# Attention and MLP of one gated block: one hand-ordered stream of work in place of three stages

## The chip, the cores and the metric

One core of one Trainium2 chip runs the kernel. The metric is the device time of one execution in microseconds. Engines are named as the profile names them: PE (matrix products), DVE (vector), ACT (activation functions), POOL and SP (here they mostly issue DMAs). PSUM is the memory that PE writes its products to; SBUF is the working memory.

## What is computed

The input x has 2048 tokens of 512 values, all tensors are bf16. Its LayerNorm goes into two branches, and the product of both is added to x:

```python
x = A_x
xn = _layernorm(x, axis=-1)
s = _A_ref(xn, A_k_cache, A_v_cache, A_wq, A_wo)
g = _silu(_B_ref(xn, B_w1, B_w2))
return x + s * g
```

Branch A is attention: q = xn @ wq gives 32 heads of 128; every 4 heads share one of 8 heads of the K and V caches, of which the last W = 512 positions are used, without a mask; scores are scaled by 128 ** -0.5, a softmax follows, p @ v, and the joined heads (4096 values) go through wo to 512 values. Branch B is an MLP: silu(xn @ w1) with 1792 inner values, then @ w2, and silu once more on the result.

## The kernel before

The 2048 tokens are four blocks of 512 (`NBLK`), each of four tiles of 128 (`BLKT`). The kernel has three stages, each with its own tile pools, and a scheduler orders the instructions of each engine.

- Start (lines 81 to 131): 16 tiles of x, K, V, w1, w2, wq and wo are loaded on SP's and POOL's queues. K is turned by PE transposes into `kT` (line 103), copied out of PSUM by DVE (104). Each tile of x gets its LayerNorm (113 to 120: statistics, a square root on ACT, reciprocal, centre and scale), four PE transposes (130) and a DVE copy (131) into `xnT`.
- MLP (133 to 166): for each block 14 products `h_ps` of four matmuls (143), a sigmoid on ACT (151) and a multiply on DVE (152) into `hT`; then for each of four tiles 14 matmuls `oB_ps` (157), sigmoid (165) and multiply (166) into `g_sb`. Both PSUM tiles have two buffers.
- Attention (168 to 240): for each block and each of 32 heads four matmuls give `qT_ps` (180), DVE casts it to `qT_s` (188); for each of four tiles one matmul gives the scores `sc_ps` of 128 by 512 (192), ACT takes exp into `e_t` and sums the row into `den` (197), DVE takes the reciprocal (199) and writes the scaled row into `p_all` (200), a view in pieces of 128. One transposing DMA on SP's queue turns `p_all` into `pT_sb` (206), four matmuls with V give `oT_ps` (212), DVE casts it into `oT_store` (219). `p_all` and `pT_sb` have two buffers, `qT_ps` and `oT_ps` one each, `sc_ps` three. After the heads of a block come four sums of 32 matmuls each, `s_ps` (224), two buffers; the scheduler lets two of them begin beside the block's heads. Their results are multiplied by `g_sb` (235), added to x (239) and stored (240).

In every matmul of the MLP, the attention and the output, 512 columns are streamed against a weight of 128 by 128.

## Time and profile before

| | us |
|---|---|
| median of 6 runs (757.45 to 763.96) | 759.74 |
| the profiled execution | 759.4 |
| its span, first to last instruction | 757.6 |
| PE busy, 2592 matmuls | 605.5 |
| DVE busy | 480.5 |
| ACT busy | 371.4 |

The span is what the trace covers; the profiled execution's own time is 1.8 us longer. Engines run beside one another, so their busy times don't add up to the span. Matmuls overlap, so their pitch, start to start, tells more than the duration of one (about 380 ns). A line such as L212 is line 212 of the kernel before. In the views of the trace "x4" is a count, "idle before" is time in which the engine stood still ahead of the instruction, and the name behind "<-" is what ended that wait. The chain of waits goes back from the last instruction to what released it, step by step; "issue" is time in which it found nothing to wait for. For DMAs, "to landing" runs from the issue to the arrival of all bytes.

### The profile page before, as it was taken

Reading aid. Unit: us, or ns where it says so; the run is one execution under the profiler, and the core shown is the slowest. Engines: PE = TensorE matmul, PEld = TensorE weight load, DVE = VectorE, ACT = ScalarE, POOL = GpSimd, SP = SyncE. Lnnn points to the kernel's source line nnn. Section 1 sums busy time; section 2 is a strip of 40 time slices with the busy share of each in tenths; the row PEclk is TensorE's granted clock in tenths of the full one; section 3 lists DMA queues with packets and bytes.
Section 4 is the critical chain, followed back from the end, with each engine's and each line's share of the span. In section 5 each row is a group of like instructions: output and inputs, shape, how many; then the busy total and the mean of one; then the engine's idle time right before and its main releaser. Section 6 shows DMA issues by size and latency. Waiting matters only on the chain.

```text
span 757.6 us, 8922 instructions
## 1 busy us (share of the span) xinstructions
PE 605.5 (80%) x2592; PEld 244.2 (32%) x2592; DVE 480.5 (63%) x1473; ACT 371.4 (49%) x1115; POOL 22.6 (3%) x40
## 2 busy tenths in 40 slices
PE   1049999988989889787777898887887978877866
PEld 1033444433333334233232343333232422323322
DVE  3274445547868763676767747767676477777741
ACT  1015344447767650565656525666565256656520
POOL 7000000000000000000000000000000100000000
PEclk9999999999999999999999999999999999999979
DMA  9960000008787883676777665667767367667740
GB/s 278 349 232 0 1 0 1 1 24 157 148 137 148 152 142 73 104 133 125 126 122 129 114 122 108 129 118 133 123 123 135 92 114 136 127 127 125 132 81 27
DMA packets 278064, 88.13 MB, mean 116 GB/s; under 512 B 271424, under 2 KB 274496, under 8 KB 277504
## 3 DMA queue, kind: packets, MB, share of 16 engines
q1 hardware_dynamic: 274976, 77.35, 54.2%
q0 software_dynamic: 3040, 10.23, 4.0%
q8 instruction: 20, 0.33, 0.2%
q14 instruction: 28, 0.23, 0.1%
HBM read 18.35 MB, written 2.10 MB: 27 GB/s over the span
## 4 chain that ended last, share of the span: by engine, by line
issue 40%; PE 25%; DMA 25%; DVE 7%; ACT 2%; POOL 1%; SPq 0%; POOLq 0%; DVEq 0%; ACTq 0%
DMA pT_sb<-p_all 20%; PE oB_ps L157 6%; PE h_ps L143 6%; PE oT_ps L212 4%; PE s_ps L224 3%; DMA k_nat<-in_A_k_cache_dram 3%; PE sc_ps L192 3%; PE qT_ps L180 2%; DMA w_sb<-in_B_w_dram 2%; DVE p_all L200 1%; DVE oT_store L219 1%; DVE qT_s L188 1%; ACT e_t L197 1%; PE xnT_ps L130 1%; DVE xnT L131 1%
## 5 line engine op out<-in xcount | busy, mean ns | idle before, releaser
L197 ACT ACTIVATE e_t<-sc_ps 128x512 bf16<-128x512 f32 x512 | 300.7, 596 | 241.7 <-PE sc_ps L192 207.1
L192 PE MATMUL sc_ps<-kT,qT_s 128*128 128x512 bf16 x512 | 160.5, 383 | 34.5 <-DVE qT_s L188 32.5
L200 DVE TENSOR_SCALAR p_all<-e_t,rden 128x512 bf16<-128x512 bf16 x512 | 172.5, 350 | 23.9 <-DMA pT_sb<-p_all 14.7
L212 PE MATMUL oT_ps<-pT_sb,v_sb 128*128 128x512 bf16 x512 | 133.9, 384 | 51.3 <-DMA pT_sb<-p_all 49.8
L180 PE MATMUL qT_ps<-xnT,wq_sb 128*128 128x512 bf16 x512 | 146.8, 382 | 2.0 <-DVE g_sb L166 1.4
L224 PE MATMUL s_ps<-wo_sb,oT_store 128*128 128x512 bf16 x512 | 136.0, 385 | 11.6 <-DVE oT_store L219 10.7
L199 DVE RECIPROCAL rden<-den 128x1 f32<-128x1 f32 x512 | 77.2, 160 | 74.1 <-ACT e_t L197 70.5
L219 DVE CAST oT_store<-oT_ps 128x512 bf16<-128x512 f32 x128 | 88.1, 688 | 36.0 <-PE oT_ps L212 35.5
L197 ACT ACTIVATION_READ_ACCUMULATOR e_t<-sc_ps 128x1 f32 x512 | 103.5, 202 | 0.0
L188 DVE CAST qT_s<-qT_ps 128x512 bf16<-128x512 f32 x128 | 87.1, 681 | 11.3 <-PE qT_ps L180 9.7
L212 PEld LDWEIGHTS <-v_sb 128*128 128x128 bf16 x512 | 49.7, 97 | 125.3 <-issue 83.8
L192 PEld LDWEIGHTS <-qT_s 128*128 128x128 bf16 x512 | 47.2, 98 | 120.5 <-DVE qT_s L188 72.4
L224 PEld LDWEIGHTS <-oT_store 128*128 128x128 bf16 x512 | 48.4, 99 | 81.9 <-DVE oT_store L219 27.9
L180 PEld LDWEIGHTS <-wq_sb 128*128 128x128 bf16 x512 | 50.3, 98 | 70.8 <-issue 17.9
L143 PE MATMUL h_ps<-xnT,w_sb 128*128 128x512 bf16 x224 | 55.0, 386 | 3.7 <-DVE hT L152 3.2
L152 DVE TENSOR_TENSOR hT<-h_ps,sig 128x512 bf16<-128x512 f32 x56 | 38.6, 691 | 29.9 <-ACT sig L151 29.9
L157 PE MATMUL oB_ps<-w_sb,hT 128*128 128x512 bf16 x224 | 53.2, 379 | 0.3 <-DVE g_sb L166 0.3
L151 ACT ACTIVATE sig<-h_ps 128x512 bf16<-128x512 f32 x56 | 33.4, 597 | 31.3 <-PE h_ps L143 31.3
L235 DVE TENSOR_TENSOR sg<-s_ps,g_sb 128x512 f32<-128x512 f32 x16 | 10.7, 688 | 41.5 <-PE s_ps L224 41.5
L143 PEld LDWEIGHTS <-w_sb 128*128 128x128 bf16 x224 | 22.0, 98 | 33.5 <-issue 10.7
L157 PEld LDWEIGHTS <-hT 128*128 128x128 bf16 x224 | 21.2, 98 | 28.1 <-DVE hT L152 2.9
L166 DVE TENSOR_TENSOR g_sb<-oB_ps,sig 128x512 bf16<-128x512 f32 x16 | 11.1, 692 | 26.6 <-ACT sig L165 26.6
(30 smaller groups left out, 106.5 us busy)
## 6 DMA issues: line engine op xcount, KB each, us to landing
wo_sb<-in_A_wo_dram POOLq DMA_DIRECT2D x1, 4096.0 KB, 34.5
wq_sb<-in_A_wq_dram SPq DMA_DIRECT2D x1, 4096.0 KB, 31.6
pT_sb<-p_all SPq DMA_TRANSPOSE x128, 4.3
w_sb<-in_B_w_dram SPq DMA_DIRECT2D x1, 1792.0 KB, 13.8
w_sb<-in_B_w_dram POOLq DMA_DIRECT2D x1, 1792.0 KB, 12.7
x_t<-in_A_x_dram SPq DMA_DIRECT2D x8, 128.0 KB, 14.1
x_t<-in_A_x_dram POOLq DMA_DIRECT2D x8, 128.0 KB, 7.7
x_e<-in_A_x_dram SPq DMA_DIRECT2D x8, 128.0 KB, 2.2
```

The source lines that it names most:

```text
L143: nc.tensor.matmul(h_ps, w1_sb[:, c, f * P : (f + 1) * P], xnT[:, c, tok0 : tok0 + BLK], start=(c == 0), stop=(c == ND - 1),)
L152: nc.vector.tensor_tensor(out=hT[:, f, :], in0=h_ps, in1=sig, op=ALU.mult)
L157: nc.tensor.matmul(oB_ps, hT[:, f, j * P : (j + 1) * P], w2_sb[:, f, :], start=(f == 0), stop=(f == NFC - 1),)
L180: nc.tensor.matmul(qT_ps, wq_sb[:, c, h * DH : (h + 1) * DH], xnT[:, c, tok0 : tok0 + BLK], start=(c == 0), stop=(c == ND - 1),)
L188: nc.vector.tensor_copy(qT_s, qT_ps)
L192: nc.tensor.matmul(sc_ps, qT_s[:, j * P : (j + 1) * P], kT[:, g_kv, :], start=True, stop=True)
L197: nc.scalar.activation(e_t, sc_ps, ACT.Exp, scale=INV_SQRT_DH, accum_out=den)
L199: nc.vector.reciprocal(rden, den)
L200: nc.vector.tensor_scalar_mul(p_all[:, :, j, :], e_t.rearrange("p (kc q) -> p kc q", q=P), rden,)
L212: nc.tensor.matmul(oT_ps, v_sb[:, g_kv, kc, :], pT_sb[:, kc, :], start=(kc == 0), stop=(kc == NKC - 1),)
L219: nc.vector.tensor_copy(oT_store[:, h, :], oT_ps)
L224: nc.tensor.matmul(s_ps, oT_store[:, h, j * P : (j + 1) * P], wo_sb[:, h, :], start=(h == 0), stop=(h == HQ - 1),)
```

## The change

The same matrix products are computed. What is new is the order, the buffers and some of the small operations:

- On PE, ACT, DVE and SP the instructions stand in the order in which the program is written (`tc.manual_schedule`). Only the first block's LayerNorm (with PE transposes, and ACT copies out of PSUM) and its MLP stand ahead of attention. The other three blocks get their statistics beside it, are centred into `xnb`, and are transposed by a DMA; K is transposed by a DMA straight out of DRAM.
- One loop then runs over 128 steps `s`, one a head. A step issues four scores, the query projection of the head two steps on, and the weighted sum of the head three steps back (`LAG`). Between them `pump` puts matmuls from a list, `fill`: in the first 32 steps those of the MLP of blocks 1 to 3 (336, some 10.5 a step), in the later 96 those of the output projection of the block before (384, four a step). The output projection of the last block follows at the end.
- exp writes straight into `p_all`, and DVE scales it there in place, two rows with one reciprocal (`normalise`). `p_all` and the transposed `pT` have three buffers.
- silu is computed with tanh: (tanh(h / 2) + 1) * h is twice silu, in one `scalar_tensor_tensor`; the factor left over is taken up in the next scale (0.25 in the last tanh and in the final sum).
- wo is not loaded at the start. Its pieces take the memory of w1 and w2 once the MLP is done with it: two of 7 heads from POOL's queue, two of 2 heads, and six small ones on SP's queue behind the transposes.
- wq, K, V, xnT and g are tiles of their own per group or block. The results are stored through POOL's queue.

```diff
-                nc.scalar.activation(sig, h_ps, ACT.Sigmoid)
-                nc.vector.tensor_tensor(out=hT[:, f, :], in0=h_ps, in1=sig, op=ALU.mult)
...
-                    e_t = p2.tile([P, W], BF16, name="e_t", bufs=3)
...
-                    nc.scalar.activation(e_t, sc_ps, ACT.Exp, scale=INV_SQRT_DH, accum_out=den)
...
-                pT_sb = p2.tile([P, NKC, BLK], BF16, name="pT_sb", bufs=2)
...
-                o_t = p2.tile([P, D], BF16, name="o_t", bufs=3)
-                nc.vector.tensor_tensor(out=o_t, in0=x_e, in1=sg, op=ALU.add)
...
+LAG = 3
+OT_BUFS = 53
+PS_BUFS = {"sc": 3, "q": 1, "o": 1, "f": 3}
...
+    reg = ctx.enter_context(tc.tile_pool(name="reg", bufs=1))
+    work = ctx.enter_context(tc.tile_pool(name="work", bufs=2))
+    ps = ctx.enter_context(tc.tile_pool(name="ps", bufs=1, space=bass.MemoryType.PSUM))
...
+    w1_sb = [reg.tile([P, ND, FH * P], BF16, name=f"w1_{i}", tag=f"big{i}") for i in range(2)]
+    w2_sb = [reg.tile([P, FH, D], BF16, name=f"w2_{i}", tag=f"big{2 + i}") for i in range(2)]
...
+        x_blk[b] = work.tile([P, BLKT, D], BF16, name="x_blk", tag="pT", bufs=3)
...
+    def mlp_units(b, tag):
+        units = []
+        cur = {}
+
+        def h_mm(f, c):
+            if c == 0:
+                cur["ps"] = ps.tile([P, BLK], FP32, name="h_ps", tag=tag, bufs=PS_BUFS[tag])
+            nc.tensor.matmul(
+                cur["ps"],
+                w1_sb[f // FH][:, c, (f % FH) * P : (f % FH + 1) * P],
+                xnT[b][:, c, :],
+                start=(c == 0),
+                stop=(c == ND - 1),
+            )
+            if c == ND - 1:
+                th = work.tile([P, BLK], BF16, name="th", bufs=2)
+                nc.scalar.activation(th, cur["ps"], ACT.Tanh, scale=0.5)
+                nc.vector.scalar_tensor_tensor(
+                    out=hT[b][f // 2][:, f % 2, :], in0=th, scalar=1.0, in1=cur["ps"], op0=ALU.add, op1=ALU.mult
+                )
...
+        def o_mm(j, f):
+            if f == 0:
...
+                nc.scalar.activation(th, cur["ps"], ACT.Tanh, scale=0.25)
...
+    def q_proj(s):
+        b, h = divmod(s, HQ)
+        q_ps = ps.tile([P, BLK], FP32, name="q_ps", tag="q", bufs=1)
...
+        qT[s] = work.tile([P, BLK], BF16, name="qT", bufs=3)
+        nc.vector.tensor_copy(qT[s], q_ps)
...
+    def score(s, j):
+        h = s % HQ
+        if j == 0:
+            p_all[s] = work.tile([P, NKC, BLKT, P], BF16, name="p_all", tag="p_all", bufs=3)
+            den[s] = work.tile([P, BLKT], FP32, name="den", bufs=3)
+        sc = ps.tile([P, W], FP32, name="sc_ps", tag="sc", bufs=3)
...
+        nc.scalar.activation(
+            p_all[s][:, :, j, :],
+            sc.rearrange("p (kc q) -> p kc q", q=P),
+            ACT.Exp,
+            scale=INV_SQRT_DH,
+            accum_out=den[s][:, j : j + 1],
+        )
...
+    def normalise(s, j0, j1):
+        rden = work.tile([P, 2], FP32, name="rden", bufs=4)
+        nc.vector.reciprocal(rden, den[s][:, j0 : j1 + 1])
+        for j in range(j0, j1 + 1):
+            nc.vector.tensor_scalar_mul(
+                p_all[s][:, :, j, :], p_all[s][:, :, j, :], rden[:, j - j0 : j - j0 + 1]
+            )
...
+    def flip(s):
+        pT[s] = work.tile([P, NKC, BLK], BF16, name="pT", tag="pT", bufs=3)
+        nc.sync.dma_start_transpose(
+            pT[s].rearrange("p kc (j q) -> p (kc j) q", q=P), p_all[s][:, :, :, :]
+        )
...
+        o_ps = ps.tile([P, BLK], FP32, name="o_ps", tag="o", bufs=1)
...
+        oT[s] = work.tile([P, BLK], BF16, name="oT", bufs=OT_BUFS)
+        nc.vector.tensor_copy(oT[s], o_ps)
...
+    def load_wo(lo, n, tag):
+        t = reg.tile([P, n, D], BF16, name=f"wo{lo}", tag=tag)
+        nc.gpsimd.dma_start(t, A_wo[ds(lo * DH, n * DH), :].rearrange("(h p) n -> p h n", p=P))
+        wo_t.append((lo, n, t))
...
+    def out_units(b):
+        units = []
+        cur = {}
+
+        def mm(j, h):
+            if h == 0:
+                cur["ps"] = ps.tile([P, D], FP32, name="s_ps", tag="f", bufs=3)
...
+            if h == HQ - 1:
+                sg = reg.tile([P, D], FP32, name="sg", tag=f"pair{2 + j % 2}")
+                nc.vector.tensor_tensor(out=sg, in0=cur["ps"], in1=g_sb[b][:, j, :], op=ALU.mult)
+                nc.vector.scalar_tensor_tensor(
+                    out=cur["x"], in0=sg, scalar=0.25, in1=cur["x"], op0=ALU.mult, op1=ALU.add
+                )
+                nc.gpsimd.dma_start(out2[ds((b * BLKT + j) * P, P), :], cur["x"])
...
+    with tc.manual_schedule(engines={ENG.PE, ENG.Activation, ENG.DVE, ENG.SP}):
+        load_x(0)
...
+        for i in range(2):
+            nc.sync.dma_start(w1_sb[i], w1v[:, :, i * FH * P : (i + 1) * FH * P])
+        load_x(1)
+        for i in range(2):
+            nc.sync.dma_start(w2_sb[i], w2v[:, i * FH : (i + 1) * FH, :])
+        load_x(2)
...
+            nc.scalar.copy(xnT[0][:, :, j * P : (j + 1) * P], t_ps)
...
+        load_x(3)
         for g in range(HKV):
...
+            nc.sync.dma_start_transpose(
+                kT[g].rearrange("p (o w) -> p o w", o=1), A_k_cache[0, g, ds(SK - W, W), :]
+            )
...
+        load_qv(range(3))
+
+        u0 = mlp_units(0, "sc")
...
+            if i == NH:
...
+                stats(3, [0, 1, 2, 3], mvs[3])
+                for b in range(1, NBLK):
+                    rstd_of(mvs[b], [0, 1, 2, 3], rss[b])
+                for b in range(1, NBLK):
+                    xnb = work.tile([P, ND, BLKT, P], BF16, name="xnb", tag="p_all", bufs=3)
+                    for j in range(BLKT):
+                        center(b, j, mvs[b], rss[b], xnb[:, :, j, :])
+                    nc.sync.dma_start_transpose(
+                        xnT[b].rearrange("p c (j q) -> p (c j) q", q=P), xnb[:, :, :, :]
+                load_qv(range(3, HKV))
...
+        fill = []
+        for b in range(1, NBLK):
+            fill += mlp_units(b, "f")
...
+        q_proj(0)
+        q_proj(1)
+        wo_state = 0
+        for s in range(NSTEP):
+            b, h = divmod(s, HQ)
+            if b >= 1 and h == 0:
+                fill += out_units(b - 1)
+            if b == 0:
+                target = (h + 1) * n_mlp // HQ
+                n = target - done
+            else:
+                n = 4
+            score(s, 0)
+            if s >= 1:
+                normalise(s - 1, 2, 3)
+                flip(s - 1)
+                if pieces:
+                    wo_piece()
+            if s + 2 < NSTEP:
+                q_proj(s + 2)
+            pump(n - n // 2 - n // 4 if n > 4 else 0)
+            score(s, 1)
+            if s >= LAG:
+                weighted(s - LAG)
+            score(s, 2)
+            normalise(s, 0, 1)
+            pump(n // 4 if n > 4 else n // 2)
+            score(s, 3)
+            pump(n - (n - n // 2 - n // 4) - n // 4 if n > 4 else n - n // 2)
+            if wo_state == 0 and done >= n_mlp - BLKT * NFC:
+                load_wo(0, 7, "big0")
+                load_wo(7, 7, "big1")
+                wo_state = 1
+            if wo_state == 1 and done >= n_mlp:
+                late = [
+                    (lo, n, reg.tile([P, n, D], BF16, name=f"wo{lo}", tag=tag))
+                    for lo, n, tag in ((14, 7, "big2"), (21, 7, "big3"))
...
+        fill += out_units(NBLK - 1)
+        s = NSTEP
+        normalise(s - 1, 2, 3)
+        flip(s - 1)
+        for i in range(LAG):
+            weighted(s - LAG + i)
+            pump(8)
+        pump(len(fill))
```

Three places in the order of the engines. First PE in the later steps. `sc_ps` are scores, `oT_ps`/`o_ps` the weighted sum, `qT_ps`/`q_ps` the query, `s_ps` the output projection; each LDWEIGHTS loads the weight of the matmul behind it. Before, from the end of one weighted sum:

```order
L212 MATMUL oT_ps<-pT_sb,v_sb 128x512
L192 LDWEIGHTS qT_s
L192 MATMUL sc_ps<-kT,qT_s 128x512
L192 LDWEIGHTS qT_s
L192 MATMUL sc_ps<-kT,qT_s 128x512
L192 LDWEIGHTS qT_s
L192 MATMUL sc_ps<-kT,qT_s 128x512
L180 LDWEIGHTS wq_sb
L180 MATMUL qT_ps<-xnT,wq_sb 128x512
```

Now, from the same point:

```order
L222 MATMUL o_ps<-pT,v_94 128x512
L193 LDWEIGHTS qT
L193 MATMUL sc_ps<-kT_87,qT 128x512
L249 LDWEIGHTS oT
L249 MATMUL s_ps<-wo_1983,oT 128x512
L249 LDWEIGHTS oT
L249 MATMUL s_ps<-wo_1983,oT 128x512
L193 LDWEIGHTS qT
L193 MATMUL sc_ps<-kT_87,qT 128x512
```

The scores that stood in a row now have two matmuls of the output projection between them, and the weighted sum ahead of them is of a head three steps back. Second, DVE in the same steps; `CAST` takes the query and the weighted sum out of PSUM, `RECIPROCAL` and `TENSOR_SCALAR` scale the probabilities. Before:

```order
L219 CAST oT_store<-oT_ps 128x512
L199 RECIPROCAL rden<-den 128x1
L200 TENSOR_SCALAR p_all<-e_t,rden 128x4x128
L199 RECIPROCAL rden<-den 128x1
L200 TENSOR_SCALAR p_all<-e_t,rden 128x4x128
L188 CAST qT_s<-qT_ps 128x512
```

Now, one whole step:

```order
L206 RECIPROCAL rden<-den 128x2
L208 TENSOR_SCALAR p_all<-p_all,rden 128x4x128 x2
L185 CAST qT<-q_ps 128x512
L226 CAST oT<-o_ps 128x512
L206 RECIPROCAL rden<-den 128x2
L208 TENSOR_SCALAR p_all<-p_all,rden 128x4x128 x2
```

The first reciprocal and the two multiplies belong to the head before; both casts now stand between the two halves of the scaling. Third, DVE at the end of the first block's MLP. `BN_STATS` and `BN_AGGR` are LayerNorm's statistics, `TENSOR_SCALAR` into `xn` or `xnb` its centring. Before, from the last centring on:

```order
L120 TENSOR_SCALAR xn<-x_t,mv,rstd 128x512
L131 COPY xnT<-xnT_ps 128x4x128
L104 COPY kT<-kT_ps 128x512
L152 TENSOR_TENSOR hT<-h_ps,sig 128x512 x14
L166 TENSOR_TENSOR g_sb<-oB_ps,sig_566 128x512
```

Now, behind the fourteen inner products:

```order
L99 BN_STATS st<-x_blk 128x6
L100 BN_AGGR mv<-st 128x2
L106 RECIPROCAL rstd<-rstd 128x4 x3
L109 TENSOR_SCALAR xnb<-x_blk,mv,rstd 128x4x128 x12
L152 SCALAR_TENSOR_TENSOR g_105<-th,oB_ps 128x512 x4
L185 CAST qT<-q_ps 128x512 x3
```

The statistics that stood ahead of the MLP (the last one of four is shown), three reciprocals and twelve centrings now stand between the last inner product of that MLP and the first of its four outputs.

## Rows read from the trace of the kernel before

**Rows 1.** Page, part 1: busy us, share of the span, count.
```profile
PE 605.5 (80%) x2592; PEld 244.2 (32%) x2592; DVE 480.5 (63%) x1473; ACT 371.4 (49%) x1115; POOL 22.6 (3%) x40
```

**Rows 2.** Stretches: length, busy PE, PEld, DVE, ACT, POOL, clock, DMA share, GB/s.
```profile
0.00:56.20 56.20, 13.23 (x96) 9.01 (x97) 27.52 (x89) 5.46 (x17) 13.87 (x24) 1.00 0.88 290
56.20:162.20 106.00, 101.08 (x449) 43.22 (x449) 49.43 (x72) 43.89 (x73) 0.00 (x0) 1.00 0.00 1
162.20:288.70 126.50, 111.69 (x457) 44.39 (x457) 93.69 (x325) 84.68 (x264) 0.55 (x1) 0.97 0.77 137
```

**Rows 3.** Page, part 5: groups, busy, mean ns of one, idle before and its releaser.
```profile
L197 ACT ACTIVATE e_t<-sc_ps 128x512 bf16<-128x512 f32 x512 | 300.7, 596 | 241.7 <-PE sc_ps L192 207.1
...
L200 DVE TENSOR_SCALAR p_all<-e_t,rden 128x512 bf16<-128x512 bf16 x512 | 172.5, 350 | 23.9 <-DMA pT_sb<-p_all 14.7
L212 PE MATMUL oT_ps<-pT_sb,v_sb 128*128 128x512 bf16 x512 | 133.9, 384 | 51.3 <-DMA pT_sb<-p_all 49.8
...
L152 DVE TENSOR_TENSOR hT<-h_ps,sig 128x512 bf16<-128x512 f32 x56 | 38.6, 691 | 29.9 <-ACT sig L151 29.9
```

**Rows 4.** Chain of waits, 205 to 245 us: start, length, what.
```profile
220.38 4.25 DMA pT_sb<-p_all
...
224.67 1.02 PE oT_ps L212 x4
225.69 0.65 PE sc_ps L192 x3
226.34 0.43 PE qT_ps L180 x2
...
227.15 4.27 DMA pT_sb<-p_all
```

**Rows 5.** The transposing DMAs: issues on SP, all landings, one stretch in flight.
```profile
220.38 5.27 SPq L206 DMA_TRANSPOSE pT_sb<-p_all  x2
...
223.74 5.29 SPq L206 DMA_TRANSPOSE pT_sb<-p_all  x2
...
DMA to landing us min/median/max: 4.2/4.3/6.4
...
222.00:224.00 2.00, 1.90 (x10) 0.78 (x9) 1.76 (x9) 1.76 (x6) 0.00 (x0) 1.00 1.16 214
```

**Rows 6.** Order of time on PE: a dense run, and the MLP's first matmuls.
```profile
289.73 13.97 PE L224 MATMUL s_ps<-wo_sb,oT_store 128*128 128x512 bf16 x64
...
56.20 3.57 PE L143 MATMUL h_ps<-xnT,w_sb 128*128 128x512 bf16 x8 [0.51 <-DVE kT L104]
```

**Rows 7.** Order of time on DVE in an attention stretch.
```profile
222.86 0.21 DVE L199 RECIPROCAL rden<-den 128x1 f32<-128x1 f32 x2
223.05 0.62 DVE L200 TENSOR_SCALAR p_all<-e_t,rden 128x512 bf16<-128x512 bf16 x2
```

**Rows 8.** The start: order of time, groups by line, and two stretches.
```profile
2.98 0.69 DVE L113 BATCH_NORM_STATS2 stats<-x_t 128x6 f32<-128x512 bf16 x1 [2.11 <-DMA x_t<-in_A_x_dram]
...
7.31 0.42 DVE L131 COPY xnT<-xnT_ps 128x512 bf16<-128x512 bf16 x1
...
L113 DVE BATCH_NORM_STATS2 stats<-x_t 128x6 f32<-128x512 bf16 x16 | 10.8, 680 | 10.4 <-DMA x_t<-in_A_x_dram 10.4
...
L120 DVE TENSOR_SCALAR xn<-x_t,mv,rstd 128x512 bf16<-128x512 bf16 x16 | 6.2, 406 | 0.1
...
10.00:20.00 10.00, 0.61 (x4) 0.34 (x4) 2.00 (x5) 0.00 (x0) 5.78 (x6) 1.00 1.06 330
20.00:40.00 20.00, 2.63 (x22) 2.19 (x23) 4.93 (x17) 0.96 (x4) 0.00 (x0) 1.00 1.04 359
```

**Rows 9.** The end, in order of time.
```profile
751.36 0.69 DVE L235 TENSOR_TENSOR sg<-s_ps,g_sb 128x512 f32<-128x512 f32 x1 [5.49 <-PE s_ps L224]
752.08 0.69 DVE L239 TENSOR_TENSOR o_t<-x_e,sg 128x512 bf16<-128x512 bf16 x1
753.07 0.55 POOL L240 DMA_DIRECT2D out_dram<-o_t  x1 [14.62 <-DVE o_t L239]
```

More of the change, by code (lines that the diff above doesn't have):

```diff
@@ L29 @@
     out: bass.AP,
-    dbg: dict | None = None,
 ):
@@ new lines, in stats, with rstd_of @@
+    def stats(b, js, mv):
+        for j in js:
+            st = work.tile([P, nc.vector.BN_STATS_DIM], FP32, name="st", bufs=4)
+            nc.vector.bn_stats(out=st, in_=x_blk[b][:, j, :])
+            nc.vector.bn_aggr(out=mv[:, j, :], in_=st)
+    def rstd_of(mv, js, rstd):
+        nc.scalar.activation(
+            rstd[:, js[0] : js[-1] + 1], mv[:, js[0] : js[-1] + 1, 1], ACT.Sqrt, bias=eps, scale=1.0
+        )
+        nc.vector.reciprocal(rstd[:, js[0] : js[-1] + 1], rstd[:, js[0] : js[-1] + 1])
@@ new lines @@
+    qT = {}
+    p_all = {}
+    pT = {}
+    oT = {}
+    den = {}
+    def q_proj(s):
+        b, h = divmod(s, HQ)
+        q_ps = ps.tile([P, BLK], FP32, name="q_ps", tag="q", bufs=1)
+        hr = h % REP
+        for c in range(ND):
+            nc.tensor.matmul(
+                q_ps,
+                wq_sb[h // REP][:, c, hr * DH : (hr + 1) * DH],
+                xnT[b][:, c, :],
+                start=(c == 0),
+                stop=(c == ND - 1),
+            )
+        qT[s] = work.tile([P, BLK], BF16, name="qT", bufs=3)
+        nc.vector.tensor_copy(qT[s], q_ps)
@@ new lines, in weighted, with wo_of @@
+    def weighted(s):
+        h = s % HQ
+        o_ps = ps.tile([P, BLK], FP32, name="o_ps", tag="o", bufs=1)
+        for kc in range(NKC):
+            nc.tensor.matmul(
+                o_ps, v_sb[h // REP][:, kc, :], pT[s][:, kc, :], start=(kc == 0), stop=(kc == NKC - 1)
+            )
+        oT[s] = work.tile([P, BLK], BF16, name="oT", bufs=OT_BUFS)
+        nc.vector.tensor_copy(oT[s], o_ps)
+        del pT[s], p_all[s], qT[s], den[s]
+    wo_t = []
+    def wo_of(h):
+        for lo, n, t in wo_t:
+            if lo <= h < lo + n:
+                return t[:, h - lo, :]
+        raise KeyError(h)
@@ new lines, with pump, wo_piece @@
+        fill = []
+        for b in range(1, NBLK):
+            fill += mlp_units(b, "f")
+        n_mlp = len(fill)
+        done = 0
+        def pump(n):
+            nonlocal done
+            for _ in range(n):
+                if fill:
+                    fill.pop(0)()
+                    done += 1
+        late = []
+        pieces = []
+        def wo_piece():
+            lo, n = pieces.pop(0)
+            t0, _, t = next(x for x in late if x[0] <= lo < x[0] + x[1])
+            nc.sync.dma_start(
+                t[:, lo - t0 : lo - t0 + n, :],
+                A_wo[ds(lo * DH, n * DH), :].rearrange("(h p) n -> p h n", p=P),
+            )
```

292 lines of the change are left out of this document (122 added, 170 removed).

## The prediction

> **What bounds the kernel now.** Busy time first [rows 1]: PE 605.5 us is the largest, but matmuls overlap, so I read their pitch in the densest stretch: 64 matmuls of the output projection in 13.97 us with the last one's 0.38 in it, (13.97 - 0.38) / 63 = 0.2157 us each [rows 6]. The kernel has 2496 matmuls of 512 columns (512 each for queries, scores, weighted sums and output, 448 for the MLP): 2496 x 0.2157 = 538.4 us. So 757.6 - 538.4 = 219 us of the span are not matmul time. The table by stage [rows 2] says where: the start takes 56.2 us before the MLP's first matmul; the MLP 106.0 us for 448 matmuls worth 96.6 (9.4 lost); from 162.2 to the end 595.4 us for 2048 worth 441.8 (153.6 lost).
>
> In the attention windows no engine is full: in the first, 126.5 us, PE shows 111.7, DVE 93.7, ACT 84.7 and the DMA share is 0.77. The wait view and the chain say why: PE waits 49.8 us for the transposed probabilities pT_sb, ACT 207 us for scores [rows 3], and in a close look the chain is a transposing DMA of 4.25 us, the weighted sum, the next head's scores, then the next such DMA, 6.77 us for two heads [rows 4]. With two buffers of p_all and pT_sb the loop through that DMA sets the pace, and PE has too little other work to put into it. It is latency, not bandwidth: the issues stand 3.4 us apart, each lands after 4.3 (median), so they overlap, and while bytes flow they flow at 214 GB/s, 524,288 bytes in 2.45 us [rows 5].
>
> **Removed work.** PE's matmuls of 512 columns all stay. 80 of 96 small PE transposes go, and all 24 PSUM copies leave DVE (four to ACT); 256 of 512 reciprocals go, since two rows now share one. All of it was off the bound or in the start.
>
> **The steady step (96 of 128 heads).** PE has 4 query, 4 score, 4 weighted and 4 output matmuls: 16 x 0.2157 = 3.45 us. DVE: 93.69 / 32 = 2.93 us a head before [rows 2], less two reciprocals at 0.1 each (two back to back take 0.21, [rows 7]), plus two instructions of 0.69 every eighth step (0.17): 2.90. ACT: 84.68 / 32 = 2.65. DMA: 2.45. PE is the longest by 0.55 us.
>
> Does the order let it run? Count a step in matmuls: scores at 0, 5, 10, 13, the query at 1 to 4, the weighted sum at 6 to 9, fill between. The fourth exp ends about 0.38 + 0.6 + 0.2 us after its matmul starts, at place 2.5 of the next step; a reciprocal and two multiplies (0.1 + 0.62, and handoffs) later, at place 6.5, the DMA is issued. Its weighted sum stands at place 6 two steps on, 31.5 places or 6.8 us later, against a landing of 4.3 (median) and 6.4 (longest of 128) [rows 5]: covered, by 2.5 and by 0.4 us. If that cover is lost PE stands still, with the two later scores of that step queued behind, and ACT and DVE dry up. The single PSUM buffers for query and weighted sum have DVE's cast done some 7 places (1.5 us) before their next use. Three p_all and three pT buffers are free a step before they are wanted.
>
> **The first 32 steps** carry the other three MLP blocks, 336 matmuls, 10.5 a step: 22.5 x 0.2157 = 4.85 us. DVE 2.73 + 1.69 evacuations x 0.69 [rows 3] = 3.9; ACT 2.65 + 1.69 x 0.6 = 3.7. PE again. Wo now arrives in these steps and the next five, 4 MB beside the transposes, at 359 GB/s [rows 8] some 12 us of DMA: the two large pieces fall where 4.85 - 2.45 = 2.4 us a step are free; the six small ones, each queued on SP behind one transpose, add up to 1.1 us to steps of 3.45 that use 2.45. Cost 0 to 8 us, taken 2.
>
> **The start.** In the trace of before the first LayerNorm tile runs from 2.98 to 7.73 us [rows 8]. Three more at DVE's pace (0.68 + 0.41 and two short ones, about 1.3) give 11.6; with only four tiles ahead of PE instead of sixteen plus K, 9.6 is possible; taken 10.5. w1 is behind 0.5 MB of x, 2.3 MB at 330 to 359 GB/s, about 10 us: its second half is wanted later. After a quiet start eight matmuls took 3.57 us [rows 6]: 8 x (0.446 - 0.216) = 1.9 us extra. K is now transposed by the DMA out of DRAM, which no row shows: between 2.9 us (1 MB at 359) and four times the 4.9 us that 214 GB/s gives, 20 us. PE wants the first query weights near 38 us, and what the queue holds up to them is 6.2 MB, 17 us at 359 GB/s, plus K: done by 23 or, at the far end, by 38. Behind them come 2 MB and the transposes of the second block's xnT, which the fill wants at 41: 0 to 5 us late, taken 0 by the nearer row, 214.
>
> At the end of the first MLP block DVE does four statistics (0.85 each) and twelve centrings (0.41) in a row, about 8.8 us, before it evacuates the next PSUM tile. PE has three buffers, 42 matmuls or 9.1 us: a stall near 1.7 (two table loads of ACT lie beside it). The first two queries then wait for one another's cast (0.69 and handoffs), 1.8 together. Sum 3.5.
>
> **In-place scaling and strides.** exp writes straight into p_all and DVE scales it there; tanh with scalar_tensor_tensor replaces sigmoid and multiply; in the program's ACT order no table load stands between tanh and exp, the last of four is ahead of the first exp. DVE's multiply already writes this strided view in 0.35 us, its cost contiguous-to-contiguous elsewhere is 0.41 [rows 3, 8], so 0.35 is kept; the far bound is the 0.69 us of operations on fp32. scalar_tensor_tensor is taken at 0.69, the row of the multiply it replaces; twice that would bring DVE to 5.0 in a first step of 4.85, about 5 us in all.
>
> **Sum.** 10.5 + 1.9 + 538.4 + 3.5 + 2 (Wo) + 0.5 (last transposes: 24 matmuls, 5.2 us, stand between the last step and the last weighted sum) + 5.4 (1% of the matmul time for handoffs; bounds 0 and the MLP stage's own, below) + 6.3 (the last matmul's end at 751.3 to 757.6, [rows 9]; this tail of two DVE operations and a store stays) = 568.5 us of span. The run of before took 759.4 for a span of 757.6, so 1.8 more: **570 us**; that run lies 0.3 under the median of 759.74.
>
> **Rivals.**
> (a) The fill doesn't fill: its matmuls wait for their own evacuation, as in the MLP stage of before, 106.0 / 448 = 0.2366 a matmul against 0.2157 [rows 2, 6]. Everywhere, 2496 x 0.0209 = 52 us, less the 5.4 counted: 617; by half, 593. Against: three buffers instead of two, and other work between.
> (b) Reading p_all strided costs DVE its fast rate: 4 x 0.34 = 1.36 us a step, 4.26 against 3.45 in 96 steps and 5.2 against 4.85 in 32: +78 + 11, 659. Against: the write of that view doesn't.
> (c) Transposes follow one another only after landing: 4.3 a step, 96 x 0.85 = +82, 652. Against: issues 3.4 us apart with landings of 4.25 [rows 5].
> (d) Slower than before: the in-order PE stops at each weighted sum because landings grow under the denser traffic. From issue to use is about two steps, so a landing L makes steps of L / 2. It costs nothing up to 6.8 us and (L / 2 - 3.45) x 96 beyond; 763 us needs 193, L = 10.9 as the mean. The longest of 128 was 6.4.
> (e) Matmuls could go denser than I count. The longest dense run in the trace shows 0.2157 us a matmul, so I give little for it. The Trainium skill (TensorE: Matmul & The Clock Gate, Back-to-back issue gap) gives about 131 ns as the sustained spacing at 512 columns in a stream of load and matmul pairs, and calls about 216 the isolated gap; by that rule the matmuls would be an estimated 327 us. DVE would then set the pace: 480.5 [rows 1] less 256 x 0.1 for reciprocals and 24 x 0.42 for copies [rows 8] is 445, and with 3 ahead and 6.3 behind it about 454. The 64 matmuls [rows 6] speak against the rule.
>
> **How the numbers follow.** The forecast, 557 to 592, 0.75: the low end is 9.6 + 1.9 + 538.4 + 6.3 + 1.8 = 558; the high end 570 + 6 (Wo at its bound) + 5 (K at its bound) + 11 (two more per cent of handoffs). (a) above that, to 617, 0.12; (b) 0.04; (c) 0.05; (d) 0.02; (e) 0.01; the last 0.01 is no change, the order undone by something unseen. The range 557 to 612 holds the forecast and most of (a), over 8 in 10. About 0.5% is what a measurement can tell from no change: faster 0.97, within 0.01, slower 0.02.
>
> **What would show it.** Right: matmul pitch near 0.216 in all stages, steps of 3.45 us from about 200 us on and of 4.85 before, DMA share near 0.7 to 0.9 in the steady steps, MLP's first matmul near 10.5 us, waits of PE for pT small. (a) shows as PE waiting for DVE or ACT on h_ps and s_ps; (b) as a scaling multiply of 0.69; (c) and (d) as PE's waits for pT, in (c) with issues 4.3 apart, in (d) with landings over 6.8. Wrong would be a first stage that ends past 20 us or a step that another engine fills.

## The result, and the profile of the changed kernel

The changed kernel takes 570.33 us (median of 8 runs, 568.58 to 571.11) beside 760.86 of the kernel before (16 runs, 757.33 to 763.96): ratio 0.7498, 95% interval 0.7482 to 0.7515. The forecast was 570 us, its range 557 to 612. The profiled execution took 570.95 us, its span is 568.8.

From the page of the changed kernel: part 1 (busy us, share of the span, count) and the groups of part 5 that answer to [rows 3].

```profile
PE 547.4 (96%) x2512; PEld 245.9 (43%) x2512; DVE 438.3 (77%) x1184; ACT 387.3 (68%) x1111; POOL 22.1 (4%) x42
...
L196 ACT ACTIVATE p_all<-sc_ps 128x512 bf16<-128x512 f32 x512 | 305.8, 598 | 107.0 <-PE sc_ps L193 99.5
...
L208 DVE TENSOR_SCALAR p_all<-p_all,rden 128x512 bf16<-128x512 bf16 x512 | 157.8, 351 | 9.1
...
L222 PE MATMUL o_ps<-pT,v 128*128 128x512 bf16 x512 | 131.8, 380 | 2.7 <-DMA pT<-p_all 2.7
...
L135 DVE SCALAR_TENSOR_TENSOR hT<-th,h_ps 128x512 bf16<-128x512 bf16 x56 | 37.7, 680 | 12.5 <-ACT th L134 12.3
```

PE went from 80% to 96% [rows 1]. The weighted sum's wait for its transposed operand went from 49.8 to 2.7 us, ACT's wait for scores from 207 to 99.5 [rows 3]. The scaling multiply in place takes 351 ns, as the one of before (350), and the scalar_tensor_tensor 680 ns where 691 stood.

The stages, in the view of stretches (columns as in [rows 2]):

```profile
10.50:40.00 29.50, 26.17 (x108) 10.74 (x106) 24.01 (x56) 14.12 (x23) 0.00 (x0) 1.00 0.89 232
40.00:200.00 160.00, 158.29 (x734) 71.60 (x732) 121.20 (x311) 113.48 (x315) 4.65 (x6) 1.00 0.71 144
200.00:300.00 100.00, 99.81 (x463) 44.85 (x461) 84.60 (x239) 76.78 (x231) 3.33 (x6) 1.00 0.90 179
300.00:400.00 100.00, 100.00 (x465) 45.32 (x463) 85.40 (x241) 77.39 (x233) 4.51 (x8) 1.00 0.84 162
```

From 300 to 400 us PE never stands, and from 400 to 500 (not shown) it is the same: 465 matmuls in 100 us are 0.215 us each, the pitch of the dense run of before [rows 6]. DVE and ACT have time left. In order of time on PE, the scores of one step to the same place of the next:

```profile
301.59 0.38 PE L193 MATMUL sc_ps<-kT,qT 128*128 128x512 bf16 x1
...
302.89 1.03 PE L222 MATMUL o_ps<-pT,v 128*128 128x512 bf16 x4
...
305.05 0.38 PE L193 MATMUL sc_ps<-kT,qT 128*128 128x512 bf16 x1
```

305.05 - 301.59 = 3.46 us: a step is its 16 matmuls and nothing else. The transposes land much as before, after 4.2, 4.3 and 6.9 us (least, median, most; 4.2, 4.3 and 6.4 in [rows 5]); what changed is that next to nothing waits for them.

**Where the 189 us came from.** Both kernels have 538.4 us of matmuls at pitch. The rest of the span was 219.2 us and is 30.4. The start gave 56.2 - 10.0 = 46.2 [rows 2], the tail behind the last matmul stayed (6.3 and 6.1), and what is lost between the first and the last matmul shrank from 156.7 to 14.3. Not all of that is PE standing still: the mean granted clock was 0.985 before and is 0.995, 11 us short of full speed in the one span and 3 in the other, so by this estimate at most some 8 us of the gain are clock. No run changes the start alone; its 46 us are read from the two traces. In order of time, the places where the 14.3 lie:

```profile
9.96 7.36 PE L125 MATMUL h_ps<-xnT,w 128*128 128x512 bf16 x24 [0.68 <-ACT xnT L303]
...
18.93 1.02 PE L125 MATMUL h_ps<-xnT,w 128*128 128x512 bf16 x4 [0.37 <-DVE hT L135]
...
28.14 9.23 PE L142 MATMUL oB_ps<-w,hT 128*128 128x512 bf16 x42
37.91 3.18 PE L142 MATMUL oB_ps<-w,hT 128*128 128x512 bf16 x14 [0.54 <-DVE g L152]
40.93 1.03 PE L177 MATMUL q_ps<-xnT,wq 128*128 128x512 bf16 x4
43.10 1.02 PE L177 MATMUL q_ps<-xnT,wq 128*128 128x512 bf16 x4 [1.15 <-DVE qT L185]
...
44.91 1.02 PE L177 MATMUL q_ps<-xnT,wq 128*128 128x512 bf16 x4 [0.57 <-DVE qT L185]
45.77 0.81 PE L125 MATMUL h_ps<-xnT,w 128*128 128x512 bf16 x3
...
535.79 1.40 PE L222 MATMUL o_ps<-pT,v 128*128 128x512 bf16 x4 [1.95 <-DMA pT<-p_all]
```

The first block's 56 matmuls of the inner products run from 9.96 to 28.14, 18.2 us for 12.1: 6.1 lost. Its 56 output matmuls take 12.8 for 12.1: 0.7. The first three queries and one score take 4.84 for 2.8: 2.0. From 45.77 to the last matmul's end at 562.7 stand 2371 matmuls, 511.4 us: 5.5 lost, most of it around the last transposes.

### The profile page after: what moved, and what is told of

Read it like the earlier page. It is cut to its first block, busy times and chain, and to the rows that moved or that the text cites. A ratio compares the mean times of both kernels' runs of the same rounds, so it can differ in the third digit from the quotient of the medians.

```text
span 568.8 us, 8091 instructions
## 1 busy us (share of the span) xinstructions
PE 547.4 (96%) x2512; PEld 245.9 (43%) x2512; DVE 438.3 (77%) x1184; ACT 387.3 (68%) x1111; POOL 22.1 (4%) x42
## 4 chain that ended last, share of the span: by engine, by line
issue 53%; PE 33%; DMA 6%; DVE 5%; POOL 2%; ACT 1%; POOLq 0%; DVEq 0%
PE h_ps L125 7%; PE oB_ps L142 7%; PE q_ps L177 6%; PE sc_ps L193 6%; PE o_ps L222 6%; DMA out_dram<-x_e 4%; DVE st L99 2%; POOL x_e L258 1%; DVE hT L135 1%; PE s_ps L249 1%; DMA pT<-p_all 1%; DVE xnb L109 1%; DVE mv L100 0%; POOL out_dram L265 0%; DMA x_blk<-in_A_x_dram 0%
## 5 line engine op out<-in xcount | busy, mean ns | idle before, releaser
L196 ACT ACTIVATE p_all<-sc_ps 128x512 bf16<-128x512 f32 x512 | 305.8, 598 | 107.0 <-PE sc_ps L193 99.5
L193 PE MATMUL sc_ps<-kT,qT 128*128 128x512 bf16 x512 | 193.2, 379 | 0.0
L208 DVE TENSOR_SCALAR p_all<-p_all,rden 128x512 bf16<-128x512 bf16 x512 | 157.8, 351 | 9.1
L249 PE MATMUL s_ps<-wo,oT 128*128 128x512 bf16 x512 | 143.7, 382 | 0.0
L222 PE MATMUL o_ps<-pT,v 128*128 128x512 bf16 x512 | 131.8, 380 | 2.7 <-DMA pT<-p_all 2.7
L177 PE MATMUL q_ps<-xnT,wq 128*128 128x512 bf16 x512 | 131.4, 379 | 1.7 <-DVE qT L185 1.7
L226 DVE CAST oT<-o_ps 128x512 bf16<-128x512 f32 x128 | 88.4, 690 | 44.9 <-PE o_ps L222 44.5
L196 ACT ACTIVATION_READ_ACCUMULATOR p_all<-sc_ps 128x1 f32 x512 | 100.5, 196 | 0.0
L185 DVE CAST qT<-q_ps 128x512 bf16<-128x512 f32 x128 | 88.2, 689 | 7.2 <-PE q_ps L177 7.2
L125 PE MATMUL h_ps<-xnT,w 128*128 128x512 bf16 x224 | 59.8, 390 | 3.5 <-DVE hT L135 2.8
```

What stands on the lines that cost most here:

```text
L125: nc.tensor.matmul(cur["ps"], w1_sb[f // FH][:, c, (f % FH) * P : (f % FH + 1) * P], xnT[b][:, c, :], start=(c == 0), stop=(c == ND - 1),)
L177: nc.tensor.matmul(q_ps, wq_sb[h // REP][:, c, hr * DH : (hr + 1) * DH], xnT[b][:, c, :], start=(c == 0), stop=(c == ND - 1),)
L185: nc.vector.tensor_copy(qT[s], q_ps)
L193: nc.tensor.matmul(sc, qT[s][:, j * P : (j + 1) * P], kT[h // REP], start=True, stop=True)
L196: nc.scalar.activation(p_all[s][:, :, j, :], sc.rearrange("p (kc q) -> p kc q", q=P), ACT.Exp, scale=INV_SQRT_DH, accum_out=den[s][:, j : ...
L208: nc.vector.tensor_scalar_mul(p_all[s][:, :, j, :], p_all[s][:, :, j, :], rden[:, j - j0 : j - j0 + 1])
```

## Experiments

Each run is beside runs of the kernel before on the same chip. Where only one time is given, it is one execution.

### The fill, and what is left without it

```diff
-            if b >= 1 and h == 0:
+            if s == 0:
+                pump(n_mlp)
+                done = n_mlp
+            if b >= 1 and h == LAG:
                 fill += out_units(b - 1)
-            if b == 0:
-                target = (h + 1) * n_mlp // HQ
-                n = target - done
-            else:
-                n = 4
+                pump(len(fill))
+            n = 0
```

> Here the MLP of blocks 1 to 3 stands in one piece in step 0 and each block's output projection in one piece behind its heads, so that a step holds only its 12 attention matmuls; order in the step, buffers and operations stay. Theory (the steps of the changed kernel are full of PE work, and what made that possible is mostly the distance of two steps between a transpose and its use): without fill a step is set by DVE, 2.73 us of work, or a little more, 2.75 to 3.0; 128 x 2.75 to 3.0 = 352 to 384, the MLP 448 x 0.2157 = 97 to 106, the output 512 x 0.2157 = 110, some 12 ahead and 8 to 12 behind and between: 580 to 625 us. Rival (the fill itself is the gain; without it the holes of the kernel before come back, 126.5 / 32 = 3.95 us a head): 128 x 3.95 = 506, sum about 735 us.

Measured: 608.0 us. So 38 us of the gain hang on the fill, and some 155 are there without it. In order of time on DVE, the same reciprocal in two steps of 12 matmuls (between them stand two multiplies, two casts, a reciprocal and two multiplies, none with a wait):

```profile
161.27 0.17 DVE L206 RECIPROCAL rden<-den 128x2 f32<-128x2 f32 x1
...
163.92 0.16 DVE L206 RECIPROCAL rden<-den 128x2 f32<-128x2 f32 x1
```

163.92 - 161.27 = 2.65 us without a gap: in such steps DVE is the bound, as expected, but its step is 2.65, not 2.73. It is not the bound in all of them: PE waits 30 times for a transpose, 22.5 us in all, 1.8 at most. The rival, 735 us, falls.

### The distance between transpose and use

```diff
-LAG = 3
-OT_BUFS = 53
+LAG = 2
+OT_BUFS = 54
...
-            st = work.tile([P, nc.vector.BN_STATS_DIM], FP32, name="st", bufs=4)
+            st = work.tile([P, nc.vector.BN_STATS_DIM], FP32, name="st", bufs=2)
```

> Here the weighted sum stands two steps behind its scores in place of three (LAG 2, one more buffer for oT, two fewer for the statistics); all else stays. Theory (the landing of a transpose, 4.3 us, is covered by the 6.8 us between its issue and its use): the cover falls by one step to 3.35 us, 15.5 matmuls; a steady step then takes 4.3 plus what stands around it, about 4.4 us in place of 3.45, 96 x 0.95 = 91 more, and the first 32 steps, 4.85 with a cover of 4.7, hardly more: about 655 us, with PE waiting for pT in nearly every later step. Rival (landings don't matter, the order and the fill alone do): 570 us, within 5.

Measured: 660.24 us, 90 more. Its wait of the weighted sums (us in all, times, longest), and three of them in order of time:

```profile
PE o_ps L222 <- DMA pT<-p_all: 71.4, 54, 3.4
```
```profile
307.29 1.04 PE L222 MATMUL o_ps<-pT,v 128*128 128x512 bf16 x4 [0.74 <-DMA pT<-p_all]
...
310.78 1.04 PE L222 MATMUL o_ps<-pT,v 128*128 128x512 bf16 x4
...
316.72 1.04 PE L222 MATMUL o_ps<-pT,v 128*128 128x512 bf16 x4 [2.31 <-DMA pT<-p_all]
```

The size is as expected, the form not quite: PE does not wait in nearly every step but 54 times, and then longer: above, a step of 3.49 us is followed by one of 5.94. The waits grew by 69 us. Each costs 0.16 more than the view counts, since the matmul ahead of it is shown with 0.38 us where its pitch is 0.22: 51 more waits, 8 us. The mean granted clock fell from 0.995 to 0.979, which is another 10 us of the span. The rival, that the order alone matters, falls.

### One buffer of p_all less

```diff
-        p_all[s] = work.tile([P, NKC, BLKT, P], BF16, name="p_all", tag="p_all", bufs=3)
+        p_all[s] = work.tile([P, NKC, BLKT, P], BF16, name="p_all", tag="p_all", bufs=2)
...
-                    xnb = work.tile([P, ND, BLKT, P], BF16, name="xnb", tag="p_all", bufs=3)
+                    xnb = work.tile([P, ND, BLKT, P], BF16, name="xnb", tag="p_all", bufs=2)
```

> The changed kernel with two buffers of p_all in place of three, order and all else unchanged. Theory (the third buffer is needed for the new order: a head's exp waits until the transpose of the head two before has landed): from the first exp of a head to its transpose's issue 22.5 places or 4.9 us, then 4.3 for the landing, together 9.2 for two heads, 4.6 in place of 3.45 in 96 steps, 110 more, 670 to 690 us, with ACT waiting for the transposes. Rival (the distance of two steps between transpose and use is what counts, not the buffer of p_all): 570 to 580.

Measured: 645.94 us, 76 more. The first exp of three heads in a row, in order of time on ACT:

```profile
301.61 0.60 ACT L196 ACTIVATE p_all<-sc_ps 128x512 bf16<-128x512 f32 x1 [2.34 <-DMA pT<-p_all]
...
304.58 0.60 ACT L196 ACTIVATE p_all<-sc_ps 128x512 bf16<-128x512 f32 x1 [0.56 <-DMA pT<-p_all]
...
309.31 0.60 ACT L196 ACTIVATE p_all<-sc_ps 128x512 bf16<-128x512 f32 x1 [2.31 <-DMA pT<-p_all]
```

The mechanism is the expected one, exp waits for the transpose that frees its buffer, but two heads take 7.7 us, not 9.2: held back, the four exps of a head run 0.57 apart instead of in the rhythm of PE's step, and the transpose goes out 3.3 us after the first of them (issues at 304.9 and 307.9), not 4.9. This rhythm makes 96 x 0.4 = 38 of the 76 us. The rest lies elsewhere: the centred blocks `xnb` use the same buffers, and the first score comes 4.8 us later (48.74 in place of 43.96); PE stands 5.55 us once ahead of 190.3, with a granted clock of 0.53 from 189 to 195; and about every eighth step takes 5.0 to 5.7 us. So the 76 us are the price of the buffer in both its uses.

### Third buffers in the kernel before

```diff
-                p_all = p2.tile([P, NKC, BLKT, P], BF16, name="p_all", bufs=2)
+                p_all = p2.tile([P, NKC, BLKT, P], BF16, name="p_all", bufs=3)
...
-                pT_sb = p2.tile([P, NKC, BLK], BF16, name="pT_sb", bufs=2)
+                pT_sb = p2.tile([P, NKC, BLK], BF16, name="pT_sb", bufs=3)
...
-                x_e = p2.tile([P, D], BF16, name="x_e", bufs=3)
+                x_e = p2.tile([P, D], BF16, name="x_e", bufs=2)
...
```

> The kernel before, with three buffers in place of two for p_all and pT_sb (paid for by one buffer less each of x_e, sg and o_t); the scheduler orders it anew. Theory (the loop of the kernel before went through two buffers and the landing of a transpose, but its scheduler still puts a weighted sum close behind its transpose): some of the waits for pT_sb go, 650 to 720 us. Rival 1 (the buffers are the whole gain of the attention stage; DVE's 2.93 us a head or PE's 12 matmuls and 4 of the output set the pace): 128 x 1.1 = 140 us less, about 620 us. Rival 2 (the order is all that matters): 750 to 760 us.

Measured: 777.11 us, above all seven runs of the kernel before beside it (760.56 to 766.99). None of the three expectations holds. The two largest waits of PE's attention matmuls, of this kernel and then of the kernel before:

```profile
PE oT_ps L212 <- DMA pT_sb<-p_all: 55.7, 69, 2.8
PE sc_ps L192 <- DVE qT_s L188: 42.7, 75, 1.0
```
```profile
PE oT_ps L212 <- DMA pT_sb<-p_all: 49.8, 72, 2.6
PE sc_ps L192 <- DVE qT_s L188: 32.5, 59, 1.0
```

A third buffer of `p_all` is worth 76 us in the new order; third buffers of `p_all` and `pT_sb` brought nothing in the old one. And there is a second wait, of scores for the cast of their query, that I had passed over. The scheduler also ordered the program anew, and three small tiles (`x_e`, `sg`, `o_t`) lost a buffer, so what cost the 13 us isn't settled.

### The same cut of PE's work in both kernels

```diff
-                for c in range(ND):
+                for c in range(ND - 1):
...
-                stop=(c == ND - 1),
+                stop=(c == ND - 2),
```

> The changed kernel with 15 in place of 16 matmuls in a steady step: the query projection leaves out one of its four chunks of the input, so the queries are incomplete; nothing else moves. Theory (PE's pitch of 0.2157 us bounds every step): 128 x 0.2157 = 27.6 us less, about 543 us, steps of 3.23 us. It also takes the cover of a transpose down by two matmuls, 0.43 us, which by 6.8 against 4.3 costs nothing. Rival (the step is set by DVE's handoffs or the transposes): 565 to 570 us.

Measured: 550.13 us, 20 less. Two steps of it in order of time, and its wait for the transposes:

```profile
305.00 1.03 PE L222 MATMUL o_ps<-pT,v 128*128 128x512 bf16 x4
...
308.23 1.03 PE L222 MATMUL o_ps<-pT,v 128*128 128x512 bf16 x4
```
```profile
PE o_ps L222 <- DMA pT<-p_all: 6.5, 8, 2.0
```

The step is 3.23 us as expected, 15 x 0.2157. What is missing of the 27.6: 3.8 us more waits for pT (6.5 against 2.7) and 0.8 that the view doesn't count for five more of them, where the pieces of wo arrive between 200 and 237 us (DMA share 1.12 from 200 to 210), and some 1.5 us from 45 to 75 us, where 133 matmuls stand for 140 at a granted clock of 0.94. About 1 us I can't place. So the step is PE's alone, and the cover of the transposes is thinner at wo than "6.8 against 4.3" sounds.

> The kernel before with the same cut as e_pe15: the query projection leaves out one of its four chunks of the input, so the queries are incomplete, and PE has 128 matmuls less, 27.6 us at 0.2157. The scheduler orders the program anew. Theory (the pace of attention there is set by the loop through the transpose, with query matmuls beside it): little of it is gained, 0 to 14 us, 745 to 760, ratio 0.98 to 1.0. Rival (PE's own work bounds the kernel before as well): 27 us less, 733 us, ratio 0.964.

Measured: 719.70 us beside 762.12, ratio 0.945 (0.9423 to 0.9476): 42 us less, more than the 27.6 that were removed. Theory and rival both fall. Its wait of scores for the cast:

```profile
PE sc_ps L192 <- DVE qT_s L188: 1.9, 4, 0.8
```

That wait, 32.5 us before, is gone. To tell whether it was the cause, the next kernel takes it away and leaves the work.

```diff
-                qT_ps = p2_ps.tile([P, BLK], FP32, name="qT_ps", bufs=1)
+                qT_ps = p2_ps.tile([P, BLK], FP32, name="qT_ps", bufs=2)
```

> The kernel before with two PSUM buffers in place of one for qT_ps, the query projection's result; the scheduler orders the program anew. It tells what stood behind the 42 us that the kernel before gained from 27.6 us less of query matmuls. Theory (a second wait in each step: scores wait 32.5 us in all for the cast of their own query, and the shorter projection let the cast come earlier): with a second buffer the next head's projection can run ahead, 15 to 32 us less, 728 to 747, ratio 0.96 to 0.98, the wait of scores for the cast near zero. Rival (the wait is slack within the loop through the transpose; what it gives back is waited for at the weighted sums): 755 to 762, ratio 0.99 to 1.0.

Measured: 717.72 us beside 760.37, ratio 0.9413 (0.9367 to 0.9459). Its waits:

```profile
PE oT_ps L212 <- DMA pT_sb<-p_all: 46.3, 64, 2.2
...
PE sc_ps L192 <- DVE qT_s L188: 1.2, 3, 0.4
```

A third wait, as it was in the kernel before:

```profile
PE s_ps L224 <- DVE oT_store L219: 10.7, 18, 0.8
```

One PSUM buffer gives the kernel before 43 us: more than the theory's 15 to 32, and the rival falls. The wait for pT_sb stays (46.3); the 31 us of the other wait did not come back there, so the two stood in series. The sums' wait for their own operand, 10.7 us before, is at most 0.5 here; with 31 that makes 41. The mean granted clock also rose, from 0.985 to 0.990, which is at most another 4 us. The scheduler's order changed with it, so buffer and order aren't told apart.

Set beside the run ahead of it, the old kernel with the shorter query, this says more. There the same wait is gone too, and PE has 27.6 us less to do, yet it took 719.70 us (ratio 0.945), no less than the 717.72 here (0.9413). With that wait away it isn't PE's work that bounds the old kernel: the wait for pT_sb is the largest of its attention matmuls in both (44.7 and 46.3 us), and the transposing DMA holds 40% of the span in this kernel's chain of waits, 20% in the kernel before. The orders differ, and the other kernel keeps the sums' wait (10.8 us), so this is a sign and no proof. The second PSUM buffer and the third buffers together, in the old order, were not run; what order alone is worth stays open.

### More work on DVE

```diff
             normalise(s, 0, 1)
+            for _ in range(1):    # 3 in the second kernel
+                nc.vector.tensor_scalar_mul(p_all[s][:, :, 0, :], p_all[s][:, :, 0, :], 1.0)
```

> The changed kernel with one redundant multiply by 1.0 in each step on DVE (one row of p_all, 128 x 512 bf16, 0.35 us), between the two halves of the scaling. Theory (the steady step is bound by PE, 3.45 us, with DVE at 2.9): 0.35 us fits into DVE's slack of 0.55: 570 us, within 2. Rival (DVE and PE together set the step, every handoff counts): 128 x 0.35 = 45 us more, 615 us.

Measured: 570.49 us, ratio to the kernel before 0.7501 (0.7467 to 0.7534): nothing lost, as expected.

> The changed kernel with three such multiplies by 1.0 in each step on DVE, 3 x 0.35 = 1.05 us. Theory (the engine with the most work sets the step, and a lost slack costs what it exceeds): DVE 2.90 + 1.05 = 3.95 us against PE's 3.45 in the later 96 steps, 48 us more; in the first 32 DVE 4.9 to 5.0 against 4.85, 3 more: about 620 us, with DVE busy all the time. Rival (other slack takes it up): 570 to 580. Rival (all of it counts): 128 x 1.05 = 134 more, 704.

Measured: 590.26 us, 20 more, between theory and first rival. DVE in order of time, one step:

```profile
301.56 0.16 DVE L206 RECIPROCAL rden<-den 128x2 f32<-128x2 f32 x1
301.76 0.62 DVE L208 TENSOR_SCALAR p_all<-p_all,rden 128x512 bf16<-128x512 bf16 x2
302.29 0.68 DVE L185 CAST qT<-q_ps 128x512 bf16<-128x512 f32 x1
302.89 0.68 DVE L226 CAST oT<-o_ps 128x512 bf16<-128x512 f32 x1
303.49 0.15 DVE L206 RECIPROCAL rden<-den 128x2 f32<-128x2 f32 x1
303.68 0.62 DVE L208 TENSOR_SCALAR p_all<-p_all,rden 128x512 bf16<-128x512 bf16 x2
304.21 0.94 DVE L396 TENSOR_SCALAR p_all<-p_all 128x512 bf16<-128x512 bf16 x3
305.07 0.16 DVE L206 RECIPROCAL rden<-den 128x2 f32<-128x2 f32 x1
```

DVE does fill the step, 3.51 us from reciprocal to reciprocal. But start to start the casts stand 0.60 apart at a duration of 0.68, the multiplies 0.27 at 0.35, and three extra ones cost 0.86, not 1.05. Without them DVE needs 3.51 - 0.86 = 2.65, as in the kernel without fill, or 2.80 with the two sums of every eighth step spread over all steps; against 3.45 its mean slack is 0.65, not 0.55. With 0.06 over in a step and 0.15 for the two sums (1.2 us in every eighth step), 96 x 0.21 = 20 us: what was measured.

### Two versions with the stalls mended

```diff
+            load_x(i + 1)                  # between the halves of w1
...
+        stats(1, [0, 1, 2, 3], mvs[1])     # ahead of the inner products
...
-        q_proj(0)                          # behind the first MLP
-        q_proj(1)
+            if i == NH + 2 * NFC - 1:      # inside its output phase
+                q_proj(0)
+            if i == NH + 3 * NFC - 1:
+                q_proj(1)
...
-            pump(8)
+            pump((8, 20, 4)[i])
```

> The changed kernel with its remaining stalls mended, the same work: statistics of block 1 ahead of the first MLP's inner products and those of block 2 at four places in it, block 3 centred later, the first two query projections inside the first MLP's output phase, block 0's output projection over three tiles at once so that the late pieces of wo are wanted later, and 8, 20 and 4 output matmuls between the last weighted sums. Theory (the rest of the time is PE at its pitch, so each stall of PE that goes is gained in full): 3 to 4 us of the inner products, 0.5 at the end of that MLP, 1.9 at the first queries, 2.7 at wo, 1.9 at the last transpose: 9 to 11 us less than 570.3, about 560 us, ratio to the kernel before 0.736. Rival (PE's stalls are slack of another engine, which is next): 567 to 571, ratio 0.747 to 0.750.

Measured: 566.50 us, ratio 0.7419 (0.7387 to 0.7451): 4 of 10 us, nearer to the rival (567 to 571) than to the theory. The view of waits shows where the rest went:

```profile
PE o_ps L222 <- DMA pT<-p_all: 3.8, 4, 1.6
PE q_ps L177 <- DVE qT L185: 1.3, 1, 1.3
```

The old stalls are gone and new ones stand in their places: 1.56 us at the first transpose, which now goes out at 49.85, behind the loads of wq and V for the groups 3 to 7; 1.25 at the second query, whose cast stands behind block 3's centring; 1.17 at wo, and 0.56 near the end.

Then, against this version:

```diff
...
+        warm_up(9)                         # matmuls on zeros, result not used
...
+            warm_up((1, 2, 0, 2)[j])       # between the PE transposes
...
-            if i in (NH, NH + NFC):
+            if i in (NH, NH + 2 * NFC):    # block 3's centring behind q_proj(0)
...
+                if s in (2, 4, 6, 8, 10):
+                    load_qv([2 + s // 2])
...
-                pieces = [(14, 2), (16, 2), (18, 2), (20, 1), (21, 2), (23, 2), (25, 2), (27, 1)]
+                pieces = [(14, 2), (16, 2)] + [(h, 1) for h in range(18, 28)]
...
-            pump((8, 20, 4)[i])
+            pump((12, 16, 4)[i])
```

> As v2, with what its trace still shows as stalls of PE taken on: 14 matmuls on zeros ahead of and between the first block's PE transposes, so that PE works before the first product of the MLP (they change no result); the first query projection ahead of the centring of block 3; wq and V of the groups 3 to 7 loaded one group at a time in steps 2 to 10; the late pieces of wo one head at a time; 12, 16 and 4 output matmuls between the last weighted sums. Theory (each stall of PE counts in full): 1.9 us at the first matmuls, 1.25 at the second query, 1.6 at the first transposes, 1.2 at wo, 0.5 at the end, 6 us less than v2's 566.5: about 561 us, ratio 0.735. Rival (the stalls move on to the next operand): 565 to 567, ratio 0.742. A rival for the first matmuls alone: they stay at a pitch of 0.43 us, 563.

Measured: 559.98 us, ratio to the kernel before 0.7367 (0.7330 to 0.7405), 1.8% below the changed kernel (the intervals of the two ratios don't meet) and the fastest of those that do the whole work. Order of time on PE at the start, and the stretch from 40 us on:

```profile
1.23 3.92 PE L302 MATMUL w_ps<-warm 128*128 128x512 bf16 x9 [1.23 <-DVE warm L297]
...
9.47 2.75 PE L125 MATMUL h_ps<-xnT,w 128*128 128x512 bf16 x12 [0.24 <-ACT xnT L318]
```
```profile
40.00:200.00 160.00, 160.00 (x743) 72.53 (x742) 124.91 (x325) 117.27 (x328) 4.64 (x6) 1.00 0.74 150
```

The span is 557.5: first product at 9.47, 538.4 of matmuls, 6.1 behind them, 3.5 us lost in between in all, where the changed kernel has 14.3. So the theory holds, and the slow pitch of the first products goes too (end of this document).

## Why the prediction was right, step by step

- **The bound named for the kernel before: incomplete.** "The loop through that DMA sets the pace" was read from the chain and from the longest wait. Third buffers in that loop brought nothing (777 us, with order and three small tiles changed too), and one in another place, PSUM for the query, 43 us: scores waited 32.5 us for the cast of their query, in series with the loop. The 570 did not rest on this, since the sum was built up from the work of the new kernel, not down from the waits of the old one. A sum of the second kind would have lacked the wait for the cast.
- **The steady step, 3.45 us: right**, shown from both sides. One PE matmul less gives 3.23 us, one DVE multiply more gives nothing, three make DVE the bound.
- **DVE at 2.90: too large**, 2.80: 2.65 by pitch and 0.15 for the sums. It cost nothing here because PE was longer. With three more multiplies a step the fault grew: taken at their duration of 0.35, these cost 0.86 by pitch in place of 1.05. A step was 0.29 shorter than expected, and over 96 steps that is 28 of the 30 us by which that run was missed.
- **Cover of the transposes: right in kind.** One step less and 90 us are lost, 91 expected. At wo it is thinner (one wait of 0.19 us in the changed kernel, up to 2.0 with 15 matmuls a step).
- **First matmul at 10.5: 9.96.** Behind it, the slow first matmuls cost 2.0 in place of 1.9 (ten take 4.34 us, the eleventh starts 4.17 behind the first). The stall ahead of the outputs cost 0.5 to 0.7 in place of 1.7: DVE's four statistics and twelve centrings took 7.6 us from start to start, where durations had given 8.8. The first queries cost 2.0 in place of 1.8.
- **Missed: statistics beside the inner products.** From start to start DVE takes 0.57 for `hT` of a product and then 0.82 for a tile of the next blocks; PE waits once 0.21 and seven times 0.37 us, a group of four matmuls takes 1.39 in place of 0.86, and the eight cost 4.1 us. I had costed these statistics only where they stand in one piece. The 1% for handoffs (5.4) covered them by luck; what is left for handoffs in the steps is about 1 us.
- **Wo 2.0: about 0.5.** The pieces do load the queues (DMA share 0.90 from 200 to 300 us), yet PE waits 0.19 there.
- **Last transposes 0.5: about 3.9.** PE waits 0.52 and 1.95 us; behind the second wait the four matmuls take 1.40 in place of 1.03, and then the clock is low (below). The 24 matmuls between, 5.2 us, were compared with a landing of 4.3 alone; the last reciprocal and multiplies ahead of the issue were left out.
- **K out of DRAM, table loads, in-place scaling: at the value taken**; no wait of PE names them. K's eight transposes hold SP's queue for 12.4 us, between the bounds of 2.9 and 20.
- **The rivals.** (a) fill waiting for its own evacuation: only in block 0's inner products, 4.1 us. (b) 351 ns: false. (c) and (d): landings 4.3 and overlapping, false at this distance; at LAG 2 PE does wait for landings, 54 times. (e) the pitch is 0.2157 over 200 us without a hole: false.

The misses were +4.1 (statistics), +3.4 (last transposes) and +0.3 (slow matmuls, first queries) one way, and -4.4 (handoffs), -1.5 (wo), -1 (stall ahead of the outputs), -0.5 (start) and -0.2 (tail) the other: that 570 was hit to the microsecond is luck, that it lies in 557 to 592 is not (the terms of the low end add up to 558).

## What to carry to other kernels

Build the time of a reordered kernel up from the pitch of its longest engine, and take the pitch on every engine, not only on the longest. Do not take the first wait of a chain for the only one: a second wait in series, at most 1.0 us each time, was 31 us in all here, and the one PSUM buffer that removed it gave 43. What pays is distance in program order with the buffers to hold it: third buffers gave nothing in the old order, and one is worth 76 us in the new one.
